# A tail reordered: rank sums begun in the last close, the first chunk turned ahead, and the last output stores issued from SyncE

## Chip, cores and metric

The kernel runs on one core of one Trainium2 chip. The metric is the device time of one execution in microseconds (us), lower is better. Beside it I use a finer measure from the profile, the **tail**: the time from the end of the last attention matmul of the last batch to the end of the span. The change touches almost nothing ahead of that point.

Names used below: PE is TensorE (matmuls) and PEld its weight loads; DVE is VectorE, ACT is ScalarE, POOL or Pool is GpSimd, SP is SyncE, which issues transfers here; a q at the end marks the engine's instruction queue. The *granted clock* is the share of its full clock that TensorE was given: 1.00 is called warm, less is called cold. To *turn* a tile is to transpose it; the *close* is the step that finishes the last tiles of `x` of a batch. A transfer has *landed* when its completion is seen. In the *closing barrier*, at the end of the program, the engines wait for each other; each of them runs an instruction called DRAIN there.

## The reference, cut to what matters

```python
# attention with squared ReLU, then a mixer (B, S, D = 8, 3136, 256; rank 32; hidden 1024)
attn = np.maximum(z @ z.transpose(0, 2, 1) / S, 0.0) ** 2
x = u_in * (attn @ v)                            # per batch
h = x.transpose(0, 2, 1) @ U @ V                 # low rank: sums over all S tokens
u = x + h.transpose(0, 2, 1)
out = u + np.maximum(u @ w_ch1, 0.0) @ w_ch2
```

One fact decides the shape of the tail: `x^T @ U` sums over all tokens, so no token of a batch can get its low-rank term before attention has finished the batch's last token. For seven batches the kernel hides this behind the attention of the next batch. For the eighth there is no next batch.

## The kernel before: the parts that matter

Tokens lie in 25 tiles of 128, grouped in seven chunks. For each batch: attention fills `x` (`close_pair`), `rank` sums `x^T U` into `t1`, `low_rank` adds `t1 V` to a chunk of `x` and turns the chunk with a DMA transpose into `uT`, `up_steps` multiplies by `w1` with a ReLU, `down_steps` multiplies by `w2`, adds `x` and stores.

```python
def rank(b):
    ps = spare()[0]
    for n in range(0, NT, 2):                    # 50 small matmuls into one PSUM tile
        ...  mm(out=ps[g * R : (g + 1) * R, :D], lhsT=U_bf[:, t, :], rhs=x_at(b, t)[:, 0], ...)
    nc.scalar.copy(out=t1_sb, in_=ps[:, :D])     # t1

def low_rank(b, c, ps=None):
    ...  mm(out=ps[h][:, k * D : (k + 1) * D], lhsT=V_bf[halves[h], ...], rhs=t1[b][halves[h], :], ...)
    for h in range(2):                           # x += t1 V
        nc.vector.tensor_tensor(out=q, in0=split(ps[h][:, : len(ks) * D]), in1=q, op=ALU.add)
    transpose(out=ut..., in_=x...)               # on SyncE's queue
    uT[c] = ut

def down_steps(b, c):
    ...  nc.vector.tensor_tensor(out=o_sb..., in0=split(ps[...]), in1=x_at(b, t, nk)[:p], op=ALU.add)
         pool_dma(out=rows(out[b])[:, t : t + nk, :], in_=o_sb[:, :nk, :])

# --- the end of the kernel, after the last batch's attention ---
last = bursts_of(B - 1)
run(late)                                        # up and down projections of batch 7's last chunk
rank(B - 1)
other = sets[opened[0] % 2]
low_rank(B - 1, 0, other)
low_rank(B - 1, 1, other)
for c in range(NC + 1):                          # ups of chunk c merged with downs of chunk c - 1
    up, down = last[c]
    if c + 2 < NC:
        up = up[:1] + [lambda c=c: low_rank(B - 1, c + 2, other)] + up[1:]
    run(_merge(up, down))
```

("Batch 7's" means the seventh of eight; its last chunk is left over on purpose, to have TensorE work in the hand-over.)

Of the kernel before, what the change touches and what calls it, by code (L numbers as in the profile page):

```python
# [42 lines left out]
def kernel(  # L43
# [11 lines left out]
    nc = tc.nc  # L55
# [45 lines left out]
    def spare():  # L101

        return sets[(opened[0] + (0 if acc else 1)) % 2]
# [19 lines left out]
    def turns(i):  # L123
        return (FIRST + i) % NT
# [7 lines left out]
    def rows(ap):  # L132
        return ap[: NF * P, :].rearrange("(p t) d -> p t d", t=NF)
# [10 lines left out]
    def group(b, c):  # L144
        n = len(chunks[c])
        flat = x_bf[:, ((XB // 4) * b + c) % (XR // 4), : n * D]
        return flat.rearrange("p (a t c) -> p a t c", a=ND, c=P)
# [145 lines left out]
    def turn(b, o):  # L293
        strip = strip_pool.tile([P, HALF, P], BF16, name="strip")
        transpose(out=strip, in_=A[o][:, P:])
        strips[b, o] = strip
# [116 lines left out]

    t1 = {}

    def rank(b):

        ps = spare()[0]
        order = [turns(i) for i in range(NT)]
        for n in range(0, NT, 2):  # L420
            for g in range(G):
                m = n + g % 2
                if m < NT:
                    t = order[m]
                    mm(  # L425
                        out=ps[g * R : (g + 1) * R, :D],
                        lhsT=U_bf[:, t, :],
                        rhs=x_at(b, t)[:, 0],
                        start=(n == 0),
                        stop=(m + 2 >= NT),  # L430
                    )
        t1_sb = small.tile([P, D], BF16, name="t1_sb")
        nc.scalar.copy(out=t1_sb, in_=ps[:, :D])
        t1[b] = t1_sb

    uT = {}

    def low_rank(b, c, ps=None):

        ts = chunks[c]  # L440
        ps = spare() if ps is None else ps
        where = [(0, 0), (1, 0)] if len(ts) == 2 else [(0, 0), (0, 1), (1, 0), (1, 1)]
        order = sorted(zip(where, ts), key=lambda e: (e[0][1], e[0][0]))
        for (h, k), t in order:
            mm(  # L445
                out=ps[h][:, k * D : (k + 1) * D],
                lhsT=V_bf[halves[h], col(t) : col(t) + P],
                rhs=t1[b][halves[h], :],
                start=True,
                stop=True,  # L450
            )
        n = len(ts)
        x = group(b, c)
        dst = x.rearrange("p a t c -> p t a c")
        for h in range(2):
            ks = [k for (g, k), _ in zip(where, ts) if g == h]
            k0 = len(ks) * h if n == 2 else 2 * h
            q = dst[:, k0 : k0 + len(ks)]
            nc.vector.tensor_tensor(out=q, in0=split(ps[h][:, : len(ks) * D]), in1=q, op=ALU.add)  # L459
        ut = ut_pool.tile([P, ND * 512], BF16, name="ut")  # L460
        ut = ut[:, : ND * n * P].rearrange("p (a w) -> p a w", a=ND)
        transpose(
            out=ut.rearrange("p a (t c) -> p (a t) c", c=P),
            in_=x.rearrange("p a t c -> p (a t c)"),
        )
        uT[c] = ut

    relus = {}

# [22 lines left out]
    def down_steps(b, c):  # L492
        pairs = []
        for t in chunks[c]:
            if pair_of(t)[0] == t:
                pairs.append([])
            pairs[-1].append(t)
        at = {}
        for t in chunks[c]:
            at[t] = sum(P if k < NF else TAIL for k in at)  # L500
        hold = {}

        def step(n, k):
            pair = pairs[n]
            if k == 0:
                hold[0] = spare()[1 - n]
            ps = hold[0]
            q = at[pair[k]]
            for ht in range(NH):
                mm(  # L510
                    out=ps[:, k * D : (k + 1) * D],
                    lhsT=relus[c][:, ht, q : q + P],
                    rhs=w2_bf[:, ht, :],
                    start=(ht == 0),
                    stop=(ht == NH - 1),
                )
            if k == len(pair) - 1:
                t, nk = pair[0], len(pair)
                o_sb = out_pool.tile([P, 2, D], FP32, name="o_sb")
                p = P if t < NF else TAIL  # L520
                nc.vector.tensor_tensor(  # L521
                    out=o_sb[:p, :nk, :].rearrange("p t (a c) -> p t a c", c=P),
                    in0=split(ps[:p, : nk * D]),
                    in1=x_at(b, t, nk)[:p],
                    op=ALU.add,
                )
                if t < NF:
                    pool_dma(out=rows(out[b])[:, t : t + nk, :], in_=o_sb[:, :nk, :])  # L528
                else:
                    pool_dma(out=out[b, NF * P :, :], in_=o_sb[:TAIL, 0, :])  # L530

        return [
            lambda n=n, k=k: step(n, k) for n in range(len(pairs)) for k in range(len(pairs[n]))
        ]

    def bursts_of(b):

        out_ = []
        for c in range(NC + 1):
            up = [lambda s=s, c=c: up_steps(c)[s]() for s in range(NH // 2)] if c < NC else []  # L540
            down = down_steps(b, c - 1) if c else []
            out_.append((up, down))
        return out_
# [152 lines left out]
    def run(steps):  # L696
        for s in steps:
            s()
# [5 lines left out]
    for b in range(B):  # L704
        more = b + 1 < B
        begin = 0 if b else 2 * NG
        bursts = bursts_of(b - 1) if b else []
        burst_at = {4: (0, 1), 8: (2, 3), 13: (4, 5), 17: (6, 7)}
        z_load, z_double, z_half, z_turn = (1, 5, 7, 10) if b else (None, 9, 11, 13)
        soon = next_at if b else next_first  # L710
        v_at = (1, 3, 4, 5, 7, 8, 10, 11, 12) if b else (8, 9, 10, 12, 14, 15, 16, 17, 18)
        v_at = dict(zip(v_at, V_PARTS))
        ahead = dict(zip((2, 3, 6, 7, 10, 11, 14), range(NC)))
        first = []
        if b == 0:
            for j, k1 in [(NT - 1, NB)] + [(j, NB if j < 3 else FIRST - j) for j in range(FIRST)]:
                first += score_steps(j, 0, k1)
        for i in range(begin, NT):
            o = turns(i)
            fill = []  # L720
            if b == 0:
                if i < z_turn:
                    n = _ceil_div(len(first), z_turn - i)
                    fill, first = first[:n], first[n:]
            else:
                fill = [s for key in own_at[i] for s in score_steps(*key)]
            if more:
                fill += [s for key in soon[i] for s in score_steps(*key)]
                if i == z_load:
                    load_z(b + 1, WHOLE)  # L730
                if i == z_double:
                    double_z(b + 1, WHOLE)
                if i == z_half:
                    turn_z(b + 1, ((FIRST, NF),))
                if i == z_turn:
                    turn_z(b + 1, ((0, FIRST),))
                if i == z_turn + 1:
                    extend_z()
                if i in v_at:
                    load_v(b + 1, v_at[i])  # L740
            main = attend_steps(b, o)
            if b and i in ahead:
                main.insert(14 if (i + (i > FIRST)) % 2 == 0 else 8, lambda c=ahead[i]: low_rank(b - 1, c))
            _spread(main, fill)
            if i + AHEAD < NT:
                turn(b, turns(i + AHEAD))
            elif more:
                turn(b + 1, turns(i + AHEAD - NT))
            if b == 0 and i in weights:
                weights[i]()  # L750
            if b and i == 0:
                rank(b - 1)
            for n in burst_at.get(i, ()) if b else ():
                up, down = bursts[n]
                if not more and n >= NC - 1:
                    late += up + (down if n == NC else [])
                    up, down = [], (down if n < NC else [])
                run(_merge(up, down))


    last = bursts_of(B - 1)
    run(late)
    rank(B - 1)
    other = sets[opened[0] % 2]
    low_rank(B - 1, 0, other)
    low_rank(B - 1, 1, other)
    for c in range(NC + 1):
        up, down = last[c]
        if c + 2 < NC:
            up = up[:1] + [lambda c=c: low_rank(B - 1, c + 2, other)] + up[1:]  # L770
        run(_merge(up, down))

# [28 lines left out]
```

## Time and profile before

| | kernel before |
|---|---|
| median of the first three runs | 1053.15 us (1050.23 to 1056.76) |
| profiled span | 1050.1 us |
| TensorE busy | 95% |
| last attention matmul ends | 981.18 us |
| tail | 68.92 us |
| of it: start of the first up group of chunk 0 | 11.14 us into the tail |
| start of the first down group of chunk 0 | 17.89 us |
| end of the last matmul | 58.45 us |
| end of the last DVE add | 59.18 us |
| from there to the end of the span | 9.74 us |

The "into the tail" figures are times of the timeline less 981.18. Ends of matmuls are modelled in the profile.

The page of the kernel before, its head and first part:

```profile
span 1050.1 us, 31112 instructions
PE 996.5 (95%) x13829; PEld 788.7 (75%) x13829; DVE 527.8 (50%) x945; ACT 616.8 (59%) x830; POOL 179.2 (17%) x332
```

TensorE bounds the kernel as a whole: it idles for only 53.6 us of the span. So a gain has to come from places where TensorE waits. Table of windows of the tail before (stretch, its length, busy us with instruction counts of PE, PEld, DVE, ACT and POOL in this order, then granted TensorE clock, DMA share, GB/s):

```profile
981.10:987.10 6.00, 5.59 (x84) 4.32 (x83) 2.08 (x3) 2.78 (x6) 0.54 (x1) 1.00 0.00 0
987.10:992.30 5.20, 1.04 (x8) 0.39 (x7) 2.57 (x4) 0.35 (x1) 0.00 (x0) 1.00 0.44 108
992.30:997.20 4.90, 4.78 (x16) 1.48 (x17) 1.29 (x2) 2.04 (x3) 0.00 (x0) 0.65 0.31 59
...
999.00:1039.60 40.60, 40.60 (x307) 28.51 (x304) 12.06 (x20) 21.61 (x25) 6.51 (x12) 1.00 0.29 88
1039.60:1050.10 10.50, 0.04 (x1) 0.00 (x0) 0.69 (x1) 0.00 (x0) 0.54 (x1) 0.71 0.13 50
```

Three stretches are bad. In the second row TensorE does 1.04 us of work in 5.2 us. In the third it looks busy, but the granted clock is 0.65: busy time alone would have hidden that. In the last row no engine works for over 9 of 10.5 us. The row of 40.6 us is full at full clock: nothing to win there.

Finer windows of the third stretch show when the clock was cold:

```profile
992.30:992.70 0.40, 0.38 (x2) 0.21 (x3) 0.00 (x0) 0.00 (x0) 0.00 (x0) 1.00 1.12 212
992.80:996.10 3.30, 3.30 (x12) 0.93 (x11) 1.29 (x2) 1.02 (x1) 0.00 (x0) 0.50 0.20 36
```

So the clock was still full when the first up matmuls began, fell to 0.50 within half a microsecond, and stayed there for about 3.4 us.

The timeline of the first two bad stretches (start, duration, engine, line, operation, shapes, count, and in brackets the idle time before it and who ended it; rows that the argument does not use, PEld above all, are left out):

```profile
985.44 1.60 PE L425 MATMUL ps<-x_bf,U_bf 128*32 128x256 bf16 x50
...
987.08 0.37 ACT L433 CAST t_sb<-ps 128x256 bf16<-128x256 f32 x1 [2.89 <-PE ps L425]
987.50 0.39 PE L445 MATMUL ps<-t_sb,V_bf 64*128 64x256 bf16 x4 [0.46 <-ACT t_sb L433]
...
987.91 1.29 DVE L459 TENSOR_TENSOR x_bf<-ps,x_bf 128x512 bf16<-128x512 f32 x2 [1.68 <-PE ps L445]
...
992.32 1.47 PE L479 MATMUL ps<-ut,w_bf 128*128 128x512 bf16 x4 [2.69 <-DMA ut<-x_bf]
...
994.26 2.84 PE L479 MATMUL ps<-ut,w_bf 128*128 128x512 bf16 x8
...
997.26 1.98 PE L479 MATMUL ps<-ut,w_bf 128*128 128x512 bf16 x8 [0.16 <-ACT relu L486]
```

This is one serial chain: rank sums, copy of t1, low-rank matmuls, two adds, a transpose, and only then the first up matmul, at 992.32. The chain of waits gives the transpose's share as 3.04 us from issue to landing:

```profile
989.23 3.04 DMA ut<-x_bf
```

After it, four up matmuls take 1.47 us; once the clock is back, four take 1.03.

The end of the kernel before, first in the timeline, then the closing barrier's instructions (line, queue, operation, count: shortest/median/longest in ns, first and last start), then what SyncE's queue waited for there (us in total, times, longest us):

```profile
1039.67 0.69 DVE L521 TENSOR_TENSOR o_sb<-ps,x_bf 128x512 f32<-128x512 f32 x1 [1.05 <-PE ps L510]
1040.66 0.54 POOL L528 DMA_DIRECT2D out_dram<-o_sb  x1 [1.21 <-DVE o_sb L521]
```

```profile
L796 POOLq DRAIN  x3: 51/98/8641, 1040.6 to 1049.8; - x3
L796 SPq DRAIN  x3: 7/7/7, 1043.5 to 1049.5; - x3
L796 PEldq DRAIN  x2: 13/974/1935, 1037.7 to 1049.6; - x2
L796 DVEq DRAIN  x2: 19/374/730, 1039.7 to 1049.6; - x2
```

```profile
SPq L796 <- PEq L796: 6.4, 2, 5.9
```

Pool's drain begins with its last store and lasts 8.64 us, to 1049.3. SyncE drains in 7 ns at 1043.5, after it has seen the store land, and then waits 5.9 us in the barrier. The wait is put down to PE's queue, but PE's own longer drain began at 1037.7, took 1.94 us and had long ended; the only thing that ends near 1049.3 is Pool's drain.

### The profile page before, as it was taken

To read this page: it belongs to the slowest core of one execution; us is meant where nothing else is said; L and a number is where in the kernel's file an instruction comes from. 1 tells how busy PE (TensorE), PEld (TensorE's weight loads), DVE (VectorE), ACT (ScalarE), POOL (GpSimd) and SP (SyncE) were. 2 spreads that over 40 slices of the span, in tenths; PEclk is the share of its full clock that TensorE was granted. 3 is DMA by queue.
4 is the path that set the end of the run, shared out by engine and by line. 5 is a ranking of instruction groups with operands and counts; after the bars stand their busy time and mean duration, and the time that the engine had idled before them with its cause. 6 is when DMAs were issued, how large, how long until landed. Compare 5 with 4: busy or idle time off the path is not lost.

```text
span 1050.1 us, 31112 instructions
## 1 busy us (share of the span) xinstructions
PE 996.5 (95%) x13829; PEld 788.7 (75%) x13829; DVE 527.8 (50%) x945; ACT 616.8 (59%) x830; POOL 179.2 (17%) x332
## 2 busy tenths in 40 slices
PE   5878999999999999999999999999999999999896
PEld 4667878787777878788777887878877787778564
DVE  4857654455544645356543565445654455442331
ACT  5957674667646676466754667466664667641253
POOL 4121212111121111211112121211212110111011
PEclk9998999999999999999999999999999999999998
DMA  9999989989897799979898998988989788679231
GB/s 167 185 180 196 165 156 194 168 166 179 153 196 158 157 175 170 170 158 169 153 183 160 169 167 146 187 173 170 169 168 180 167 154 151 139 139 179 49 99 62
DMA packets 417174, 168.71 MB, mean 161 GB/s; under 512 B 392768, under 2 KB 402640, under 8 KB 417040
## 3 DMA queue, kind: packets, MB, share of 16 engines
q1 hardware_dynamic: 386464, 96.77, 59.3%
q0 software_dynamic: 30576, 69.96, 28.7%
q8 instruction: 108, 1.77, 0.7%
q14 instruction: 26, 0.21, 0.1%
HBM read 61.88 MB, written 25.69 MB: 83 GB/s over the span
## 4 chain that ended last, share of the span: by engine, by line
PE 77%; DMA 10%; ACT 4%; issue 3%; DVE 3%; POOL 1%; SPq 0%; POOLq 0%; ACTq 0%; DVEq 0%
PE ps L333 41%; PE ps L510 15%; PE ps L479 13%; PE ps L260 6%; DMA ut<-x_bf 4%; DMA strip<-A 3%; DMA zT<-z_bf 3%; ACT A L273 3%; PE ps L425 1%; ACT relu L486 1%; PE ps L445 1%; DVE A L275 1%; DVE both L348 1%; DVE x_bf L459 1%; PE ps L367 1%
## 5 line engine op out<-in xcount | busy, mean ns | idle before, releaser
L273 ACT ACTIVATE A<-ps 128x832 bf16<-128x832 f32 (+8 forms) x469 | 351.1, 764 | 178.8 <-PE ps L260 159.2
L333 PE MATMUL ps<-v,A 64*128 64x256 bf16 x4864 | 335.7, 271 | 3.4 <-DVE both L348 2.0
L275 DVE TENSOR_TENSOR A<-A 128x832 bf16<-128x832 bf16 (+8 forms) x469 | 239.4, 523 | 146.4 <-ACT A L273 143.6
L333 PE MATMUL ps<-v,strip 64*128 64x256 bf16 x4420 | 308.2, 269 | 0.0
L486 ACT ACTIVATE relu<-ps 128x1024 bf16<-128x1024 f32 (+2 forms) x224 | 202.6, 917 | 140.6 <-PE ps L479 140.6
L333 PEld LDWEIGHTS <-A 64*128 64x128 bf16 x4864 | 242.7, 94 | 44.2 <-issue 11.6
L333 PEld LDWEIGHTS <-strip 64*128 64x128 bf16 x4420 | 224.8, 94 | 30.5
L479 PE MATMUL ps<-ut,w_bf 128*128 128x512 bf16 (+2 forms) x896 | 203.5, 354 | 13.1 <-DMA ut<-x_bf 6.8
L521 DVE TENSOR_TENSOR o_sb<-ps,x_bf 128x512 f32<-128x512 f32 (+1 forms) x104 | 69.7, 670 | 277.1 <-PE ps L510 277.1
L510 PE MATMUL ps<-w_bf,relu 128*128 128x256 bf16 x1600 | 204.7, 273 | 0.0
L510 PEld LDWEIGHTS <-relu 128*128 128x128 bf16 x1600 | 156.1, 98 | 46.2 <-issue 0.8
L260 PE MATMUL ps<-zT 64*128 64x416 bf16 (+10 forms) x933 | 154.8, 318 | 20.9 <-DMA zT<-z_bf 18.3
L479 PEld LDWEIGHTS <-w_bf 128*128 128x128 bf16 x896 | 85.0, 98 | 79.2 <-issue 17.4
L317 POOL DMA_DIRECT2D u_sb<-in_u_dram x96 | 53.4, 557 | 455.5 <-DVE x_bf L357 418.4
L528 POOL DMA_DIRECT2D out_dram<-o_sb x96 | 52.4, 546 | 339.2 <-DVE o_sb L521 339.2
L347 ACT COPY both<-ps 128x512 f32<-128x512 f32 (+1 forms) x104 | 58.8, 567 | 82.8 <-PE ps L333 73.3
L348 DVE TENSOR_TENSOR both<-ps,both 128x512 f32<-128x512 f32 (+1 forms) x104 | 69.2, 666 | 30.1 <-ACT both L347 29.7
L260 PEld LDWEIGHTS <-zT 64*128 64x128 bf16 x933 | 52.0, 95 | 30.0 <-DMA zT<-z_bf 18.6
L459 DVE TENSOR_TENSOR x_bf<-ps,x_bf 128x512 bf16<-128x512 f32 (+1 forms) x112 | 65.4, 625 | 15.8 <-PE ps L445 15.8
L357 DVE TENSOR_TENSOR x_bf<-both,u_sb 128x512 bf16<-128x512 f32 (+1 forms) x104 | 69.8, 671 | 3.6
L195 POOL DMA_DIRECT2D v<-in_v_dram x61 | 34.2, 568 | 0.0
L445 PE MATMUL ps<-t_sb,V_bf 64*128 64x256 bf16 x200 | 24.2, 273 | 3.3 <-DVE x_bf L459 1.1
(39 smaller groups left out, 173.1 us busy)
## 6 DMA issues: line engine op xcount, KB each, us to landing
u_sb<-in_u_dram POOLq DMA_DIRECT2D x96, 256.0 KB, 4.1
out_dram<-o_sb POOLq DMA_DIRECT2D x96, 256.0 KB, 2.4
v<-in_v_dram POOLq DMA_DIRECT2D x57, 192.0 KB, 5.2
strip<-A SPq DMA_TRANSPOSE x196, 5.4
z_c<-in_z_dram POOLq DMA_DIRECT2D x7, 384.0 KB, 5.9
w_bf<-in_moe_w_ch_dram POOLq DMA_DIRECT2D x2, 512.0 KB, 8.2
u_sb<-in_u_dram POOLq DMA_DIRECT2D x16, 64.0 KB, 3.9
ut<-x_bf SPq DMA_TRANSPOSE x56, 5.0
```

What stands on the lines that cost most here:

```text
L260: mm(out=ps[:, k, :n], lhsT=zT[halves[k], j, :], rhs=zT_flat[halves[k], c : c + n], start=True, stop=True,)
L273: nc.scalar.activation(out=dst, in_=src, func=AF.Relu, scale=sc)
L275: nc.vector.tensor_tensor(out=dst, in0=dst, in1=dst, op=ALU.mult)
L333: mm(out=acc[t0][h][:, (o - t0) * D : (o - t0 + 1) * D], lhsT=w[halves[h]], rhs=v_both[b % 2][halves[h], j, :], start=start, stop=stop, **kw,)
L347: nc.scalar.copy(out=both[:, :w], in_=banks[1][:, :w])
L348: nc.vector.tensor_tensor(out=both[:, :w], in0=banks[0][:, :w], in1=both[:, :w], op=ALU.add)
L357: nc.vector.tensor_tensor(out=x_at(b, t0, n), in0=split(both[:, :w]), in1=u_sb[:, :n, :].rearrange("p t (a c) -> p t a c", c=P), op=ALU.mult,)
L459: nc.vector.tensor_tensor(out=q, in0=split(ps[h][:, : len(ks) * D]), in1=q, op=ALU.add)
L479: mm(out=ps[:, i, :w], lhsT=w1_bf[:, db, (hp + i) * P : (hp + i + 1) * P], rhs=uT[c][:, db, len(chunks[c]) * P - w :], start=(db == 0), st ...
L486: nc.scalar.activation(out=relus[c][:, hp : hp + 2, :w], in_=ps[:, :, :w], func=AF.Relu)
L510: mm(out=ps[:, k * D : (k + 1) * D], lhsT=relus[c][:, ht, q : q + P], rhs=w2_bf[:, ht, :], start=(ht == 0), stop=(ht == NH - 1),)
L521: nc.vector.tensor_tensor(out=o_sb[:p, :nk, :].rearrange("p t (a c) -> p t a c", c=P), in0=split(ps[:p, : nk * D]), in1=x_at(b, t, nk)[:p] ...
```

## The change

Its intent: begin the rank sums during the last close; turn the first chunk's raw `x` early, and add the low-rank term to the *turned* chunk, so that no transpose stands between t1 and the first up matmul; issue the last batch's stores from SyncE. The diff, cut to its core (`...` marks what is left out; most comments are mine):

```diff
-    def rank(b):
-        ps = spare()[0]
+    def rank(b, ps, n0=0, n1=NT):
-        for n in range(0, NT, 2):
+        for n in range(n0, n1, 2):
 ...
+        if n1 < NT:
+            return                       # first part of the sums: no copy of t1 yet
+    def turn_x(b, c): ...                # the transpose, taken out of low_rank
+    def mix(b, c):
+        ps = pair_psum()
+        for db in range(ND):             # (t1 V) already turned: two 512-column matmuls
+            mm(out=ps[:, db, :], lhsT=t1[b][halves[db], db * P : (db + 1) * P],
+               rhs=V_bf[halves[db], c0 : c0 + 512], start=True, stop=True)
+        nc.vector.tensor_tensor(out=uT[c], in0=ps, in1=uT[c], op=ALU.add)
-    def low_rank(b, c, ps=None):
+    def low_rank(b, c, ps=None, turned=True):
 ...
+                store = pool_dma if b + 1 < B else nc.sync.dma_start
 ...
+            elif i == NT - AHEAD:
+                turn_x(b, 0)             # during the last batch's attention
 ...
-    run(late)
-    rank(B - 1)
-    low_rank(B - 1, 0, other)
-    low_rank(B - 1, 1, other)
+    rank(b, other[0], 0, NT - 3)         # 44 of the 50 matmuls
+    run(late[: NH // 2])
+    rank(b, other[0], NT - 3)            # the other six, and t1
+    run(late[NH // 2 : NH // 2 + 1])
+    mix(b, 0)
+    run(late[NH // 2 + 1 :])
+    low_rank(b, 1, other)
     for c in range(NC + 1):
         up, down = last[c]
         if c + 2 < NC:
-            up = up[:1] + [lambda c=c: low_rank(B - 1, c + 2, other)] + up[1:]
+            up.insert(3 if c == 0 else 1, lambda c=c: low_rank(b, c + 2, other))
+        if c == 0:
+            up.insert(1, lambda: low_rank(b, 0, other, False))
         run(_merge(up, down))
```

More of the change, by code (lines that the diff above doesn't have):

```diff
@@ L436, with turn_x @@
     uT = {}
-    def low_rank(b, c, ps=None):
+    def turn_x(b, c):
+        n = len(chunks[c])
+        ut = ut_pool.tile([P, ND * 512], BF16, name="ut")
+        ut = ut[:, : ND * n * P].rearrange("p (a w) -> p a w", a=ND)
+        transpose(
+            out=ut.rearrange("p a (t c) -> p (a t) c", c=P),
+            in_=group(b, c).rearrange("p a t c -> p a (t c)"),
+        )
+        uT[c] = ut
+    def mix(b, c):
+        ps = pair_psum()
+        c0 = col(chunks[c][0])
+        for db in range(ND):
+            mm(
+                out=ps[:, db, :],
+                lhsT=t1[b][halves[db], db * P : (db + 1) * P],
+                rhs=V_bf[halves[db], c0 : c0 + 512],
+                start=True,
+                stop=True,
+            )
+        nc.vector.tensor_tensor(out=uT[c], in0=ps, in1=uT[c], op=ALU.add)
+    def low_rank(b, c, ps=None, turned=True):
         ts = chunks[c]
@@ L459, in low_rank @@
             nc.vector.tensor_tensor(out=q, in0=split(ps[h][:, : len(ks) * D]), in1=q, op=ALU.add)
-        ut = ut_pool.tile([P, ND * 512], BF16, name="ut")
-        ut = ut[:, : ND * n * P].rearrange("p (a w) -> p a w", a=ND)
-        transpose(
-            out=ut.rearrange("p a (t c) -> p (a t) c", c=P),
-            in_=x.rearrange("p a t c -> p (a t c)"),
-        )
-        uT[c] = ut
+        if turned:
+            turn_x(b, c)
     relus = {}
@@ L526, in step @@
                 )
+                store = pool_dma if b + 1 < B else nc.sync.dma_start
                 if t < NF:
-                    pool_dma(out=rows(out[b])[:, t : t + nk, :], in_=o_sb[:, :nk, :])
+                    store(out=rows(out[b])[:, t : t + nk, :], in_=o_sb[:, :nk, :])
                 else:
-                    pool_dma(out=out[b, NF * P :, :], in_=o_sb[:TAIL, 0, :])
+                    store(out=out[b, NF * P :, :], in_=o_sb[:TAIL, 0, :])
         return [
@@ L751 @@
             if b and i == 0:
-                rank(b - 1)
+                rank(b - 1, spare()[0])
             for n in burst_at.get(i, ()) if b else ():
@@ L758 @@
                 run(_merge(up, down))
-    last = bursts_of(B - 1)
-    run(late)
-    rank(B - 1)
+    b = B - 1
+    last = bursts_of(b)
     other = sets[opened[0] % 2]
-    low_rank(B - 1, 0, other)
-    low_rank(B - 1, 1, other)
+    rank(b, other[0], 0, NT - 3)
[5 more added lines that the diff above has]
+    low_rank(b, 1, other)
     for c in range(NC + 1):
```

## The prediction

> **What bounds the kernel.** TensorE: 95% busy (page, part 1) and 77% of the chain of waits. The change touches only the last batch's tail, from 981.1 us (last attention matmul) to 1050.1 us (end of span), 69 us of 1050. The timeline shows three losses there.
>
> 1. Serial hand-over, 985.4 to 992.3. Rank sums 1.6 us, t1 copy to 987.46, low-rank matmuls 0.4, two DVE adds 1.3 (to 989.2), then the transpose, 3.04 us to landing. 5.2 us hold 1.0 us of matmuls (windows).
> 2. A cold clock after it: granted 0.65 in 992.3-997.2; up matmuls of 512 columns start every 0.43 us instead of 0.22. Extra cost some 2.5 us. This agrees with the Trainium skill, "TensorE: Matmul & The Clock Gate", Part 1 (half rate after an idle window of about 3.4 us).
> 3. The end. The last DVE add ends at 1040.36, Pool issues the last store at 1040.66, its landing releases SyncE at about 1043.5, but Pool's own drain at the closing barrier runs 8.64 us, to 1049.3. So 9.7 us follow the last add, about 6 of them the drain alone.
>
> Between 1000 and 1039.7 TensorE is busy 39.6 of 39.7: nothing to win.
>
> **The change, step by step.**
> - 44 of 50 rank matmuls run straight after attention (their x is ready at 977.9) and cover the last close. The other six follow the late ups. One wait less (0.4 us).
> - The transpose of chunk 0's raw x is issued four tiles earlier, while SyncE is idle: off the path.
> - Added: two 512-column low-rank matmuls (0.2-0.4 us) and one DVE add of 1024 columns (estimate 1.2 us from 0.65 for 512). They replace 0.4 + 1.3 + 3.04 us on the path, and the second half of the late downs (0.9 us) covers most of the add.
> - New wait: chunk 0's ordinary low-rank matmuls, now after the first up group, wait for chunk 1's DVE adds, queued behind the mix add and a late output add: about 1 us of TensorE idle.
> - I place the first up of chunk 0 at about 987.5 (was 992.3), all warm, and the first down of chunk 0 at about 993.9 (was 999.07): 5.2 us gained, carried unchanged through the busy stretch; last matmul near 1034.4.
> - Twelve stores go from Pool to SyncE. SyncE has seven transposes of 1.2 us there, in DVE's order: no store is held long. Pool's last DMA is then near 988 and its drain hides under the projections. After the last add (about 1035.1): issue and landing some 2.4 us (the Pool stores took 2.0 to 3.0), then about 0.9 of barrier: 1038.5. Gain here: about 6.3 us.
>
> Total 11.5 us: 1053.15 - 11.5 = **1041.6 us**, range 1037.5 to 1046. Chances: over 2% faster 0.03, within 2% 0.95, over 2% slower 0.02.
>
> **What would show it.** No TensorE wait for the ut transpose in the tail; granted clock 1.0 from 981 to the last matmul; a wait of about 1 us of low-rank matmuls for DVE x_bf near 989; last matmul about 5 us earlier; Pool's drain starting near 988 and no longer last; 3 to 4 us from the last add to the end instead of 9.7.
>
> **What would make it wrong.** Slow SyncE issues that delay transposes or hold back the two output buffers; stores slower to land there; a SyncE drain as long as Pool's; a longer stall at the new DVE queue that cools the clock.

## The result

| | before | after |
|---|---|---|
| median of four runs | 1054.77 us (1050.23 to 1056.76) | 1040.05 us (1038.71 to 1041.03) |
| ratio | | 0.9866, 95% interval 0.9828 to 0.9903 |
| profiled span | 1050.1 us | 1036.8 us |
| last attention matmul ends | 981.18 | 979.48 |
| tail | 68.92 | 57.32 |
| first up group of chunk 0, into the tail | 11.14 | 6.64 |
| first down group of chunk 0 | 17.89 | 12.67 |
| last matmul ends | 58.45 | 53.23 |
| last DVE add to end of span | 9.74 | 3.36 |

Ratios are the mean time of one kernel's runs over that of the other's of the same rounds, so not quite the ratio of the medians quoted. All runs here that were timed in rounds are of the fast state (a single run's state is unknown); the class is "same" at the 2% mark, and the gain is clear of noise.

The page of the kernel after:

```profile
span 1036.8 us, 31117 instructions
PE 996.2 (96%) x13831; PEld 789.1 (76%) x13831; DVE 529.5 (51%) x946; ACT 616.6 (59%) x830; POOL 172.0 (17%) x319
```

TensorE does the same work (996.2 against 996.5 us): what went is waiting. Windows of the tail after, same columns:

```profile
979.40:985.40 6.00, 5.69 (x85) 4.08 (x84) 1.94 (x3) 3.02 (x6) 0.00 (x0) 1.00 0.00 0
985.40:990.60 5.20, 4.68 (x29) 1.80 (x27) 3.87 (x7) 2.33 (x3) 0.55 (x1) 1.00 0.41 101
...
993.00:1032.70 39.70, 39.70 (x299) 27.79 (x297) 12.05 (x20) 20.67 (x24) 0.00 (x0) 1.00 0.35 98
1032.70:1036.80 4.10, 0.01 (x1) 0.00 (x0) 0.69 (x1) 0.00 (x0) 0.00 (x0) 1.00 0.30 116
```

The stretch that held 1.04 us of matmuls in 5.2 us now holds 4.68, the granted clock is 1.00 throughout, and the end is 4.1 us instead of 10.5. The timeline of the hand-over after (those rows that the argument uses):

```profile
979.41 1.39 PE L424 MATMUL ps<-x_bf,U_bf 128*32 128x256 bf16 x44
...
983.70 0.37 ACT L434 CAST t_sb<-ps 128x256 bf16<-128x256 f32 x1
...
984.41 0.39 PE L454 MATMUL ps<-V_bf,t_sb 64*128 64x512 bf16 x2
...
984.84 1.22 DVE L461 TENSOR_TENSOR ut<-ps,ut 128x1024 bf16<-128x1024 f32 x1 [3.29 <-PE ps L454]
...
986.12 1.02 PE L499 MATMUL ps<-ut,w_bf 128*128 128x512 bf16 x4
986.58 1.28 DVE L484 TENSOR_TENSOR x_bf<-ps,x_bf 128x512 bf16<-128x512 f32 x2
...
987.32 0.27 PE L470 MATMUL ps<-t_sb,V_bf 64*128 64x256 bf16 x1 [0.17 <-DVE x_bf L484]
...
987.91 0.38 PE L470 MATMUL ps<-t_sb,V_bf 64*128 64x256 bf16 x3 [0.33 <-DVE x_bf L484]
...
988.22 1.90 PE L499 MATMUL ps<-ut,w_bf 128*128 128x512 bf16 x8
```

The mix add (L461) takes 1.22 us and the first up group follows it at once, at 986.12; four up matmuls take 1.02 us, so the clock never cooled. The new wait is visible too: chunk 0's ordinary low-rank matmuls (L470) wait at 987.3 and 987.9 for chunk 1's adds, which queue on DVE behind the mix add and a late output add. The end after: timeline, closing barrier, and the stores' median time from issue to landing (last column, us; Pool's row holds the seven earlier batches, SyncE's the last one):

```profile
1032.75 0.69 DVE L541 TENSOR_TENSOR o_sb<-ps,x_bf 128x512 f32<-128x512 f32 x1 [1.05 <-PE ps L530]
```

```profile
L827 POOLq DRAIN  x3: 51/98/7584, 986.9 to 1036.5; - x3
L827 SPq DRAIN  x3: 7/7/7, 1035.9 to 1036.2; - x3
```

```profile
out_dram<-o_sb POOLq DMA_DIRECT2D x84, 256.0 KB, 2.4
...
out_dram<-o_sb SPq DMA_DIRECT2D x12, 256.0 KB, 2.0
```

The same twelve stores of the last batch in the kernel before, from Pool:

```profile
out_dram<-o_sb POOLq DMA_DIRECT2D x12, 256.0 KB, 2.3
```

Pool's drain still takes 7.58 us, but it starts at 986.9 and is over 40 us before the end. SyncE's drain stays at 7 ns although SyncE has just issued stores.

### The profile page after: what moved, and what is told of

Same layout as the page of the kernel before. It is cut to its first block, busy times and chain, and to the rows that moved or that the text cites. A ratio compares the mean times of both kernels' runs of the same rounds, so it can differ in the third digit from the quotient of the medians.

```text
span 1036.8 us, 31117 instructions
## 1 busy us (share of the span) xinstructions
PE 996.2 (96%) x13831; PEld 789.1 (76%) x13831; DVE 529.5 (51%) x946; ACT 616.6 (59%) x830; POOL 172.0 (17%) x319
## 4 chain that ended last, share of the span: by engine, by line
PE 84%; DMA 7%; ACT 4%; DVE 3%; issue 1%; POOL 0%; SPq 0%; ACTq 0%; DVEq 0%; POOLq 0%
PE ps L333 42%; PE ps L530 17%; PE ps L499 15%; PE ps L260 6%; DMA zT<-z_bf 4%; DMA ut<-x_bf 3%; ACT A L273 2%; ACT relu L506 1%; PE ps L367 1%; PE ps L424 1%; PE ps L470 1%; DVE x_bf L484 1%; DVE A L275 1%; DVE both L348 1%; DMA v<-in_v_dram 0%
## 5 line engine op out<-in xcount | busy, mean ns | idle before, releaser
L549 POOL DMA_DIRECT2D out_dram<-o_sb x84 | 45.9, 546 | 296.2 <-DVE o_sb L541 296.2
L470 PE MATMUL ps<-t_sb,V_bf 64*128 64x256 bf16 x200 | 24.0, 271 | 2.3 <-DVE x_bf L484 0.5
```

## The experiments

**Theory.** Two gains that add: (A) the hand-over, 5.2 us, of which part is waiting and part is the cold clock that the waiting causes; (B) the end, 6.4 us, which is Pool's closing drain and not the speed of the store. **Main rivals:** B is a faster store path; A comes mostly from the early rank sums; the slow matmuls after the wait are not the clock. Since the time ahead of the tail differs from run to run (last attention matmul at 977.9 to 987.4 us in the profiles below), I judge by the tail; the timed ratios only confirm.

| run | tail | first up | first down | last matmul | last add to end | ratio to before |
|---|---|---|---|---|---|---|
| before | 68.92 | 11.14 | 17.89 | 58.45 | 9.74 | |
| after | 57.32 | 6.64 | 12.67 | 53.23 | 3.36 | 0.9866 |
| e1 stores only | 62.85 | 11.14 | 18.25 | 58.82 | 3.30 | 0.9932 [0.9900, 0.9964] |
| e2 hand-over only | 63.65 | 6.65 | 12.67 | 53.23 | 9.69 | 0.9947 [0.9915, 0.9978] |
| e3 before, wait filled | 67.37 | 11.15 | 16.36 | 56.93 | 9.71 | 0.9983 [0.9946, 1.0019] |
| e5 last 1 store on SyncE | 61.82 | 6.64 | 12.67 | 53.23 | 7.85 | one run |
| e6 last 2 | 59.11 | 6.64 | 12.67 | 53.23 | 5.15 | one run |
| e7 last 4 | 57.37 | 6.64 | 12.67 | 53.23 | 3.41 | one run |
| e8 no early turn | 60.77 | 9.79 | 16.19 | 56.75 | 3.29 | one run |
| e9 rank sums late | 58.04 | 8.04 | 13.47 | 54.03 | 3.28 | one run |
| e4 tuned | 56.26 | 6.23 | (reordered) | 52.27 | 3.26 | 0.9886 [0.9839, 0.9933] |
| e10 after again | 57.28 | 6.65 | 12.67 | 53.24 | 3.31 | 0.9914 [0.9883, 0.9946] |
| e11 tuned again | 56.35 | 6.23 | (reordered) | 52.26 | 3.36 | 0.9875 [0.9844, 0.9906] |

All kernels gave correct results.

### e1: the stores alone

```diff
 (kernel before)
+                store = pool_dma if b + 1 < B else nc.sync.dma_start
-                    pool_dma(out=rows(out[b])[:, t : t + nk, :], in_=o_sb[:, :nk, :])
+                    store(out=rows(out[b])[:, t : t + nk, :], in_=o_sb[:, :nk, :])
```

> The kernel before with only its last batch's stores moved to SyncE. Tail = from the end of the last attention matmul to the end of the span: 68.9 us before, 57.3 after the change. My theory (Pool's closing drain was last, the two parts add): tail 62.5 us, ratio 0.994, last DVE add to the end of the span 3.3 us instead of 9.7, last matmul unmoved at 58.4 us into the tail. Rival (the parts overlap: stores on SyncE are worth little while the hand-over is serial, or they come at the cost of the transposes on the same queue): tail over 65 us, or the last matmul more than 1 us later than 58.4.

Tail 62.85 us, 6.07 less than before; 3.30 us from the last add to the end. The last matmul came 0.37 us later than before. The delay arises in the cold stretch (first up group unmoved at 11.14, first down group 0.36 us later), ahead of the first store of that batch on SyncE, so it is not the stores' doing. A window of e1 shows what it is:

```profile
986.30:993.00 6.70, 3.79 (x12) 1.16 (x13) 2.53 (x4) 1.02 (x1) 0.00 (x0) 0.50 0.42 78
```

Here the clock was cold from the start of the first up group (989.0) on, for about 4.1 us of it; in the kernel before, for about 3.4. The extra 0.7 us at half clock are worth about 0.35. The theory holds.

### e2: the hand-over alone

```diff
 (kernel after)
-                store = pool_dma if b + 1 < B else nc.sync.dma_start
+                store = pool_dma
```

> The kernel after with the last batch's stores put back on Pool. My theory: tail 63.7 us (68.9 less 5.2), ratio 0.995; last matmul 53.2 us into the tail as in the kernel after; 9.6 us from the last DVE add to the end. Rival (a faster end of the matmuls is lost because Pool issues its stores late or piles them up): last matmul or last add later than in the kernel after by over 1 us.

Tail 63.65 us, 5.27 less than before; last matmul at 53.23, as in the kernel after, and 9.69 us from the last add to the end. The parts add: 6.07 + 5.27 = 11.34 us, against 11.60 for both; the missing 0.26 us are near the 0.37 us that e1's longer cold stretch cost.

### e5, e6, e7: how many stores have to leave Pool

```diff
 (kernel after; k = 1, 2, 4; the last batch has 13 stores)
-                store = pool_dma if b + 1 < B else nc.sync.dma_start
+                stored[0] += b + 1 == B
+                store = nc.sync.dma_start if stored[0] > 13 - k else pool_dma
```

> The kernel after, but of the last batch's 13 stores only the last one is on SyncE, 12 are on Pool. My theory (what is saved at the end is Pool's drain, which runs some 7.6 to 8.6 us from Pool's last issue): Pool's last issue is 1.7 us earlier than with all on Pool, so 7.5 to 8.0 us from the last DVE add to the end. Rival (the store itself is issued and lands faster through SyncE's queue): 3.4 us from the last add to the end, as with all 13 on SyncE.

> The same with the last two stores on SyncE. My theory: Pool's last issue is 4.4 us before that of all on Pool, so 5 to 6 us from the last add to the end. Rival: 3.4 us.

> The same with the last four stores on SyncE. My theory: Pool's last issue is over 10 us before the last add, so the drain is hidden: 3.4 us from the last add to the end, tail 57.3 us, as good as all 13. Rival: no difference between this, one and two stores on SyncE. If Pool's drain is set by something else than the time of its last issue, all three keep 9 us or more.

From the last add to the end: 7.85, 5.15 and 3.41 us. All three have their last store on SyncE, so a faster store path cannot tell them apart; only the time of Pool's last issue does. Pool's drain, in the closing barriers of e5, e6 and e7 in this order:

```profile
L830 POOLq DRAIN  x3: 51/93/8557, 1039.0 to 1048.0; - x3
```

```profile
L830 POOLq DRAIN  x3: 51/93/8476, 1037.3 to 1046.2; - x3
```

```profile
L830 POOLq DRAIN  x3: 51/93/8319, 1024.8 to 1038.1; - x3
```

Start plus length is 1047.6, 1045.8 and 1033.1; the spans end at 1048.3, 1046.5 and 1038.4. In the first two the end follows the drain by 0.7 us, in the third the drain is done 1.2 us before the last add begins. The rival falls: taking the last four stores off Pool gives the whole of part B. The direct difference between the two store paths is small here: 2.0 us to landing against 2.3 for the last batch's 256 KB stores. Why the drain takes 7.6 to 8.6 us, and why it is a little shorter when fewer stores came shortly before, stays open.

### e3: the wait kept, the clock kept warm

```diff
 (kernel before)
+    def fill(n):
+        ps = pair_psum()
+        for _ in range(n):
+            mm(out=ps[:, 0, :], lhsT=w1_bf[:, 0, :P], rhs=w1_bf[:, 0, :512], start=True, stop=True)
     low_rank(B - 1, 0, other)
+    fill(3)
     low_rank(B - 1, 1, other)
+    fill(11)
```

> The kernel before with 3 + 11 idle 512-column matmuls (result unused) in the wait for the first transpose, so that the wait stays and only the clock is kept warm. My theory: the cold clock is a cost of its own, about 1.8 us of the 5.2 us of the hand-over; granted clock 1.0 in the 5 us after the wait, the up matmuls start every 0.22 us, the first down group starts 16.1 us into the tail instead of 17.9; tail 67.1 us, ratio 0.998. Rival (the slow matmuls after the wait come from something else, such as memory traffic of the two transposes that are under way): spacing stays 0.43 us and the tail stays at 68.9 us or grows.

The first up group still starts at 11.15 us, so the wait is unchanged. Three lines of its timeline and one of its windows:

```profile
992.08 1.04 PE L479 MATMUL ps<-ut,w_bf 128*128 128x512 bf16 x4 [0.21 <-DMA ut<-x_bf]
...
993.37 1.94 PE L479 MATMUL ps<-ut,w_bf 128*128 128x512 bf16 x8
...
995.52 1.94 PE L479 MATMUL ps<-ut,w_bf 128*128 128x512 bf16 x8 [0.21 <-ACT relu L486]
```

```profile
992.10:997.00 4.90, 4.69 (x23) 1.86 (x24) 1.29 (x2) 3.39 (x4) 0.00 (x0) 1.00 0.48 89
```

Four up matmuls now take 1.04 us instead of 1.47, and eight take 1.94 instead of 2.84, with the granted clock at 1.00. The first down group comes 1.53 us sooner and the tail is 1.55 us shorter, with two transposes under way as before. So the clock is a cost of its own, and useless matmuls remove it. The size is below my 1.8, and the record bounds it: about 3.4 us at 0.50 are at most 1.7 us of lost work. From the start of the first up group to the end of the third it is 4.78 us before and 3.23 here, 1.55 less. The fourth waits about as long for a ReLU in both (0.16 and 0.21 us), so the ReLUs are not what made it smaller. The timed ratio alone (0.9983, interval across 1) could not have shown this.

### e8: without the early turn

```diff
 (kernel after)
-            elif i == NT - AHEAD:
-                turn_x(b, 0)
-    mix(b, 0)
+    low_rank(b, 0, other)
-            up.insert(1, lambda: low_rank(b, 0, other, False))
```

> The kernel after without the early turn and without the low-rank term added to the transpose: chunk 0 gets its low-rank add and is then transposed as before, but still between the two late down groups, with the rank sums split as in the change. My theory (turning ahead takes the 3.0 us transpose off the path, less the 1.2 us of stall that it brings at the DVE queue): first up group of chunk 0 at 9.7 us into the tail instead of 6.6, first down group 2 us later than the kernel after (14.7 instead of 12.7), tail 59.3 us if the clock stays warm, 61 us if the wait of 2.8 us is enough to cool it. Rival (most of the hand-over's gain comes from the rank sums covering the last close, not from turning ahead): tail under 58.3 us.

Tail 60.77 us, 3.45 more than the kernel after; first up group at 9.79 as expected, first down group at 16.19. That is the "cooled" branch. One timeline line and one window of e8:

```profile
993.52 4.29 PE L499 MATMUL ps<-ut,w_bf 128*128 128x512 bf16 x12 [2.71 <-DMA ut<-x_bf]
```

```profile
996.00:998.00 2.00, 2.00 (x9) 0.49 (x7) 0.00 (x0) 1.18 (x2) 0.00 (x0) 0.50 0.00 0
```

After an idle time of 2.71 us the clock came down to 0.50, again only after the matmuls had resumed (1.00 in 993.5 to 994.5, 0.50 in 994.6 to 998.0). So most of the hand-over's gain needs the early turn: 3.5 of 5.2 us are lost without it, partly as waiting and partly as clock.

### e9: rank sums in one piece, late

```diff
 (kernel after)
-    rank(b, other[0], 0, NT - 3)
-    run(late[: NH // 2])
-    rank(b, other[0], NT - 3)
-    run(late[NH // 2 : NH // 2 + 1])
-    mix(b, 0)
-    run(late[NH // 2 + 1 :])
+    run(late)
+    rank(b, other[0])
+    mix(b, 0)
     low_rank(b, 1, other)
```

> The kernel after with the rank sums in one piece behind all late ups and downs, as in the kernel before; the early turn, the mix and the stores stay. My theory (the split hides the t1 copy and the mix add behind late work, but the late output add then no longer stands in the DVE queue): first up group of chunk 0 about 1.3 us later than in the kernel after (7.9 us into the tail), the wait of chunk 0's low-rank matmuls shorter by 0.7, tail about 58.0 us. Rival (the early rank sums are the larger part of the hand-over gain): tail over 60 us.

Tail 58.04 us (58.0 expected), first up group 1.40 us later, last matmul 0.80 later than in the kernel after. Undoing the early rank sums costs 0.8 us, not the larger part. This run undoes two things at once, the split of the sums and the place of the late work around the mix; their shares were not separated.

### e4, e10, e11: the remaining waits taken out

```diff
 (kernel after)
+    run(late[:2])
     rank(b, other[0], 0, NT - 3)
-    run(late[: NH // 2])
+    run(late[2 : NH // 2])
 ...
-    run(late[NH // 2 + 1 :])
     low_rank(b, 1, other)
+    run(late[NH // 2 + 1 :])
 ...
-            up.insert(3 if c == 0 else 1, lambda c=c: low_rank(b, c + 2, other))
+            up.insert(4 if c == 0 else 1, lambda c=c: low_rank(b, c + 2, other))
-            up.insert(1, lambda: low_rank(b, 0, other, False))
-        run(_merge(up, down))
+            up.insert(2, lambda: low_rank(b, 0, other, False))
+        run((down[:1] if c == 1 else []) + _merge(up, down[c == 1 :]))
```

> The kernel after with its remaining waits taken out: the first 44 rank matmuls after two of the late up groups instead of before them, chunk 1's low-rank adds ahead of the late output add, chunk 0's ordinary low-rank after its second up group, chunk 2's after the fourth, chunk 0's first down group ahead of chunk 1's first up group. My theory (the new DVE queue cost 1.2 us and the late ups 0.65 us of TensorE idle): tail 55.6 us, 1.7 us under the kernel after; ratio to before near 0.986 to 0.984. Rival (ScalarE's ReLU chain sets the pace there, so moving the low-rank matmuls only moves the wait): tail 57 us or more.

Tail 56.26 us: 1.06 us under the kernel after, where I expected 1.7 and the rival 0.3 or less. I had sized the waits by gaps between timeline rows, about 1.2 and 0.65 us, but those gaps hold matmuls that have to run anyway. The waits of TensorE in the tail of the kernel after name the size better (us in total, times, longest us):

```profile
PE ps L470 <- DVE x_bf L484: 0.5, 2, 0.3
PE ps L499 <- ACT relu L506: 0.3, 1, 0.3
```

Both lines are gone in the tuned version, and their sum of 0.8 us is near the 0.96 us by which its last matmul is earlier. Since two of its six runs lay at 1048 to 1050 us, I ran it again beside the kernel after:

> The kernel after once more, beside the tuned version on one chip. My theory (the tail repeats to about 0.1 us, the stretch before it does not): last matmul 53.2 us into the tail, tail 57.3 to 57.4 us; total anywhere between 1036 and 1048. Rival (the tail itself varies from run to run): tail off by over 0.5 us.

> The tuned version again. My theory: last matmul 52.3 us into the tail, tail 56.3 us, 1.1 us under the kernel after; in the totals this is smaller than the spread of the runs, so the ratios to before of the two kernels overlap. Rival (the tuned order is really slower in some executions, as two of its six runs at 1048 to 1050 us may hint): tail over 57.3 us in this profile, or a median over 3 us above that of the kernel after.

The tails repeat to within 0.1 us (57.28 and 56.35). The totals do not: the unchanged kernel after had a median of 1040.05 us in the first job and 1046.25 here; the tuned one 1039.06 and 1040.34. The intervals to before overlap, as expected (0.9883 to 0.9946 against 0.9844 to 0.9906), and the rival falls: the tuned order was not slower. But the median of the kernel after is 5.9 us above the tuned one's, far more than the 0.9 us of the tails. What varies is the stretch ahead of the tail: the last attention matmul ended at 979.48 and 985.12 us in the two profiles of the same kernel. So the tuned version is about 1 us better by its tail, and its apparent lead beyond that is not explained by the tail. The copies of t1 narrow it down: from the seventh batch's copy, early in the last batch's attention, to the last attention matmul it takes 110.73 to 110.74 us in all thirteen profiles, while that copy itself comes at 867.1 to 876.7 us. So the scatter is complete before the last batch's attention gets going; its cause was not pursued.

## Why the prediction was right

The prediction was 1041.6 us; the four runs had a median of 1040.05, within its range, and the class (within 2%) was right. Point by point:

- **The hand-over.** Predicted 5.2 us, carried unchanged through the busy stretch. Measured 5.22 at the first down group (17.89 - 12.67) and 5.22 at the last matmul (58.45 - 53.23); e2 shows it alone, and no wait of TensorE for that transpose is left in the tail. Without the early turn 3.5 us of it are lost (e8), without the early rank sums and the late work around the mix 0.8 (e9); the other 0.9 were not separated. The hit to 0.02 us is partly luck: the first up group came 0.3 us later than placed (6.64 us into the tail against 987.5 - 981.18 = 6.32), and the stretch from there to the first down group was 0.4 us shorter (6.03 against 993.9 - 987.5 = 6.4).
- **The mix add.** Estimated 1.2 us for 1024 columns, measured 1.22.
- **The cold clock.** The mechanism is shown by e3. Its size was off: "some 2.5 us" in the prediction, 1.5 measured. 2.5 is about what twelve up matmuls lose if each takes 0.43 us instead of 0.22, but the clock was cold for only about 3.4 us; the prediction's own 0.65 over 4.9 us allows 1.7. The sum did not suffer, since the hand-over was counted from positions in the timeline and not by adding this term. Of the 5.22 us, 4.50 are the earlier start of the first up group (11.14 - 6.64). From there to the first down group it takes 6.75 us before, 5.21 in e3 and 6.03 after: the warm clock gives back 1.5, and the low-rank work that the change moved in there, with its wait, takes 0.8 of it.
- **The new wait on DVE.** Predicted about 1 us of idle, and too large: 0.5 us of recorded wait, in two pieces of up to 0.3.
- **The end.** Predicted 6.3 us by hiding Pool's drain, measured 6.38 (9.74 - 3.36). e5 to e7 show that it is the drain. SyncE's drain did not grow. (Thirteen stores moved; the prediction counts the twelve of 256 KB.)
- **The total.** Predicted gain in the tail 11.5 us, measured 11.6. The first comparison of runs gave more: 1.34% of before's 1054 us is 14.1 us. The second gave 0.86%, 9.1 us. The tail lies between them, and each interval includes it (11.6 of 1054 is a ratio of 0.989); the rest is the scatter ahead of the tail. That the total came within 1.6 us is therefore partly luck: the same kernel's median in the second job, 1046.25 us, is just above the predicted range.

## What to carry to other kernels

Judge a change of one stage by landmarks of that stage in the profile: here the tail repeats to 0.1 us while totals of one kernel differ by 8 us. Look at what the closing barrier waits for; a queue that drains slowly should get its last work early, and it is enough to move the last few transfers. When a serial hand-over is unavoidable, take the long link (here a transpose) off it by linearity, turning the raw data early and adding a turned correction, and count the cold clock after a wait as part of its price, for as long as the clock record shows it cold.

## What the Trainium skill lacked or had wrong

- The Trainium skill, "VectorE: DVE Perf Modes", The DRAIN you can't avoid, knows two kinds of drain in a profile: the flush after a VectorE operation, and the runtime's own before and after a program, constant at about 12 ns on all five engines. The closing drains here belong to a line of kernel.py (L796 before, L827 after), and Pool's fits neither kind: it took 7.58 to 8.64 us in all thirteen profiles and set the end of the kernel before; SyncE's took 7 ns. "DMA: Bandwidth & Descriptors" does not mention such a cost of issuing from Pool late in a program.
- The Trainium skill, "TensorE: Matmul & The Clock Gate", Part 1, puts cooling after an idle window of about 3.4 us, and its section Why this matters for your kernels sets the limit at about 3 us. Shorter waits were followed by a granted clock of 0.50 here: 2.69 us in the kernel before, 2.71 in e8, and 2.11 in e6 (at 437.7 us). A wait of 2.39 us in e2 (at 507.4 us) was not, and in e1 the clock fell by 986.3, as the wait of 2.69 us began, after a stretch with 0.93 us of matmuls in 2.4. So the length of one wait does not settle it in these runs. They agree with the page in that the slow state was half rate (0.50) and in that keeping the array busy prevented it (e3).
- The Trainium skill, "DMA: Bandwidth & Descriptors", Latency and other measured facts, gives first bytes of about 0.6 us for SyncE's path and 1 us for Pool's. Landing times of the last batch's 256 KB stores agree in direction: 2.0 against 2.3 us. Its fit for Pool, 2.0 us plus the bytes at 436 GB per second (section Anatomy of one DMA), would give 2.6 us for this size, an estimate from that page; the runs are below it.
